# A chunked scan and a bilinear feed-forward on one core: the order of the first loads, the first products and some small work changed

## The chip, the core and the metric

The kernel runs on one core of one Trainium2 chip. A core has five engines with queues of their own: PE (TensorE, matrix products, with its weight loads shown as PEld), DVE (VectorE), ACT (ScalarE), POOL (GpSimd) and SP (SyncE, which here only issues transfers). Instructions of one engine start in the order of its queue; between engines they wait on semaphores. Transfers (DMAs) issued by POOL go through one queue, those issued by SP and ACT through two others, and the same 16 DMA engines serve all three. The metric is the device time of one execution in microseconds (us), and the median over several executions is compared.

## The reference

The inputs are x (4 batches, 8 heads, 768 tokens, 32 values), a decay a per token and head, and B and C (16 values per token and head). A state space scan is computed in chunks, then a feed-forward with two products and an elementwise product between them:

```python
for c in range(nc):
    cum = np.cumsum(la, axis=-1)                       # la = log a, of the chunk
    L = np.exp(cum[:, :, :, None] - cum[:, :, None, :]) * causal
    CB = np.einsum('bhin,bhjn->bhij', Cc, Bc)
    y_intra = np.einsum('bhij,bhjd->bhid', CB * L, xc)
    y_inter = np.einsum('bhin,bhnd->bhid', Cc, state) * np.exp(cum)[..., None]
    y[:, :, sl] = y_intra + y_inter
    ...
    state = decay_full * state + sum_j(B_j x_j decay_from_j)
x = y.transpose(0, 2, 1, 3).reshape(B * S, H * D)      # 3072 x 256
return (x @ w_a) * (x @ w_b) @ w_out                   # 256 -> 1536 -> 256
```

## The kernel before, in words

The kernel works in chunks of 128 tokens: six blocks (0 to 5) of 128 tokens, and in each block two pairs of batches, so that pair p = 2 x block + 0 or 1. All orders are written out by hand: the Python code records instructions in the order in which every engine is to run them, and each engine takes its own of them in that order. The program's end (lines 768 to 1026) is that order.

The decay of a chunk is a running product Pr (`scan`, L237, DVE), taken relative to its value in the middle of the chunk (`over_mid`, L240; `sel_over_mid`, L243). The factors that B and C are multiplied with come from it in three ways:

- Block 0: small products on PE (`factors_mm`, L258) that turn Pr, then a reciprocal on DVE into fB. `scale_bc` (L328) multiplies B and C into bm and cm, `transposes` (L372) turns them on PE, and ACT and DVE copy them out (L383, L388).
- Block 1 on (C and B in tiles cq and bq, loaded by `load_q`, L155): `mid_rows` (L275) makes Ps, `turned_rows` (L284, a DVE transpose) turns it into Pt, `batch_factors` (L290, copies on ACT) spreads it by batch into FC, and `batch_inverse` (L296, a DVE reciprocal) makes FB. `scale_q` (L341, POOL) writes C times FC or B times FB into one of three planes; `prep(p)` does both, C first. `turn` (L354, DVE) transposes a plane. Here the second index of FC and FB counts blocks from 1.
- The bm that the state needs in later blocks use fBl, made by `late_factors` (L300, L301).

For each pair, `scores` (L400) makes the products of C and B on PE in the four PSUM banks SC; `mask` multiplies them with the causal table, either on DVE (L445) or, by_pool, as a copy tmp on ACT (L442) and a product on POOL (L443). The products with x (scaled to f16 by `scale_x`, L315 on ACT or L317 on POOL) give y: `pv_u` and `pv1` (L454) for pairs 0 and 1, `outputs` (L533, L481, L469) later. `ds_mm` (L508, L497), `state_sums` (L567, L569) and `spread` (L573, L583) carry the state on.

The feed-forward of block 0 goes pair by pair. A unit (`unit_mm`, L595) makes products of 256 columns with Wa into a bank aps and with Wb into a bank bps; ACT copies aps out to asb (`evac_a`, L609), and DVE multiplies (`times`, L619) into hk. `out_mm` (L634) multiplies hk with Wo, and ACT copies the result out (L646). From block 1 on a unit covers four batches: `bunit` (L664, L676, hkb) and `bout` (L690, L702). The banks of PSUM that the units take are read one by one from the string BANKS (L22 to L25), four of them, numbered 0 to 3.

The loads: SP and ACT issue a, and B and C of pairs 0 and 1 (L185 to L195). POOL issues, one after the other, x of pair 0 (two transfers), the first half of Wa, the first half of Wb, x of pair 1 (two transfers), the second half of Wa (L220 to L226), later the second half of Wb and both halves of Wo (`load_wo`, L180), with other work of POOL between them. SP issues cq and bq of block 1 once the first half of Wa has landed (L814), then B of pairs 2 and 3, x of pairs 2 and 3 (after the first half of Wo, L857), then cq and bq of block 2 and so on. Each of its transfers also waits for the one issued eight before it.

While PE has nothing to do in the head, `warmup` (L230) puts in products of zeros: six of 512 columns and two of 128 at the very start (L768, L769), ahead of `factors_mm`, and a few at later places.

Of the kernel before, what the change touches and what calls it, by code (L numbers as in the profile page):

```python
# [19 lines left out]
YS = 16.0  # L20

BANKS = (  # L22
    "012313123123123012301230123021032110321032103210321031230120312031230213012301203213021302"
    "1301203120312031201320132013201320132013201320312031203120312031203120312031203120312"
)  # L25

# [2 lines left out]
def kernel(  # L29
# [13 lines left out]
    nc = tc.nc  # L43

    nb, H, S, D = x.shape
# [14 lines left out]
    NT = NBLK - PJ // NBP  # L60
# [102 lines left out]
    def load2(eng, p, which):  # L163
        if p < P2:
            return [load1(eng, p, which, bt) for bt in range(2)]
        blk, bp = divmod(p, NBP)
        src = (B, C, x)[which][2 * bp : 2 * bp + 2, :, blk * Q : (blk + 1) * Q, :]
        return [
            eng.dma_start(
                by_token(pair_in[p][which]).rearrange("p t h n -> p (t h) n"), src.rearrange("t h q n -> q (t h) n")  # L170
            )
        ]

    def load_w(half, W):
        src = moe_w_a if W is Wa else moe_w_b
        c = slice(half * KC, (half + 1) * KC)
        return nc.gpsimd.dma_start(W[half], src.rearrange("(f p) e -> p f e", p=128)[:, :, c])

    def load_wo(half):
        return nc.gpsimd.dma_start(  # L180
            Wo[:, 6 * half : 6 * half + 6].rearrange("p (g kk) e -> p g (kk e)", kk=3),
            moe_w_out.rearrange("(g p kk) e -> p g (kk e)", p=128, kk=3)[:, 2 * half : 2 * half + 2],
        )
# [36 lines left out]
    for p in range(2):  # L220
        for bt in range(2):
            load1(nc.gpsimd, p, 2, bt)
        if p == 0:
            w0 = load_w(0, Wa)
            load_w(0, Wb)
    load_w(1, Wa)  # L226

    def warmup(n, bank, cols=512):
        for _ in range(n):
            nc.tensor.matmul(  # L230
                bank[:, 0:cols], warm[:, 0:128], warm[:, 0:cols], start=True, stop=True, skip_group_check=True
            )
# [50 lines left out]
    def turned_rows(lo, hi):  # L283
        nc.vector.transpose(  # L284
            Pt[:, lo:hi].rearrange("p k s c -> p (k s) c"), Ps[:, lo:hi].rearrange("p k (i s) -> p k s i", s=4)
        )

    def batch_factors(lo, hi, *bs):
        for b in bs:
            nc.scalar.copy(  # L290
                FC[32 * b : 32 * b + 32, lo:hi].rearrange("p k s h -> p (k s) h"),
                Pt[:, lo:hi].rearrange("p k s (b h) -> p (k s) b h", b=nb)[:, :, b],
            )
# [25 lines left out]
    def scale_bc(p, which, eng, factor=None):  # L319
        blk, bp = divmod(p, NBP)  # L320
        name, f = (("bm", fB), ("cm", fC))[which]
        if p >= P2:
            f = (fBl, fCl)[which][:, blk - P2 // NBP].rearrange("p (b t h) -> p b t h", b=NBP, t=2)[:, bp]
        else:
            f = f[:, blk, :, bp]
        raw = by_token(pair_in[p][which]) if p >= P2 else pair_in[p][which].rearrange("p h r n -> p r h n")
        m_ = mid.tile([128, 2, H, N], f16, name=name, tag=name)
        eng.tensor_tensor(  # L328
            out=m_,
            in0=raw,  # L330
            in1=(f if factor is None else factor).unsqueeze(3).broadcast_to((128, 2, H, N)),
            op=ALU.mult,
        )
        st.setdefault(p, {})[name] = m_
# [59 lines left out]
    def scores(p):  # L394
        s = st[p] if p < PJ else st["U", p]
        BT, CT = s["BT"], s["CT"]
        s["T1"] = mid.tile([128, 4, 4, Q], f16, name="t1", tag="t1")

        def score(o_, b_, c_, at):
            nc.tensor.matmul(o_, b_, c_, start=True, stop=True, skip_group_check=True, tile_position=at)  # L400

        if p >= P2:
            for j, b in itertools.product(range(4), range(nb)):
                rows = slice(32 * b, 32 * b + 32)
                score(SC[b][:, j * Q : j * Q + Q], BT[rows, j], CT[rows, j // 2], (32 * b, 0))
            return
        for e, r, m, bt in itertools.product(range(2), range(2), range(4), range(2)):
            c0 = (e * 2 + r) * Q
            o_ = SC[m][64 * bt : 64 * bt + 64, c0 : c0 + Q]
            if p >= PJ:  # L410
                bp, g = divmod(m, 2)
                row = 32 * (2 * bp + bt)
                rows = slice(row, row + 32)
                b_ = BT[rows, 2 * g + e].rearrange("p (i r) -> p r i", r=2)[:, r]
                score(o_, b_, CT[rows, g], (row, 64 * bt))
            else:
                rows = slice(32 * m, 32 * m + 32)
                score(o_, BT[rows, e, r, bt], CT[rows, bt], (32 * m, 64 * bt))
# [72 lines left out]
    def ds_mm(p, DS):  # L491
        s, bp = st[p], p % NBP
        st["DS", p // NBP] = DS
        DS = DS.rearrange("p (g d) -> p g d", d=2 * D)
        for bt, g in itertools.product(range(2), range(4)) if p >= P2 else ():
            row = 32 * (2 * bp + bt)
            nc.tensor.matmul(  # L497
                DS[row : row + 32, g],
                s["bm"][:, bt, 2 * g : 2 * g + 2, :].rearrange("p h n -> p (h n)"),
                by_token(s["X16"])[:, bt, 2 * g : 2 * g + 2].rearrange("p h d -> p (h d)"),  # L500
                start=True,
                stop=True,
                skip_group_check=True,
                tile_position=(0, row),
            )
        for r, g, bt in itertools.product(range(2), range(4), range(2)) if p < P2 else ():
            k, row = slice(64 * bt, 64 * bt + 64), 32 * (2 * bp + bt)
            nc.tensor.matmul(  # L508
                DS[row : row + 32, g],
                s["bm"][k, r, 2 * g : 2 * g + 2, :].rearrange("p h n -> p (h n)"),  # L510
                s["X16"][k, 2 * g : 2 * g + 2, r, :],
                start=(r == 0 and g == 0),
                stop=(r == 1),
                skip_group_check=True,
                tile_position=(64 * bt, row),
            )
# [106 lines left out]
    def unit(p, k2, between=None, by_pool=False):  # L623
        a_ps = unit_mm(p, k2, Wa)
        if between:
            between()
        b_ps = unit_mm(p, k2, Wb)
        asb = evac_a(a_ps)
        return lambda: times(p, k2, b_ps, asb, by_pool)
# [92 lines left out]
    def go(*items):  # L722
        for p, k2 in items:
            unit(p, k2)()

    def prep(p):
        if p < NP:
            scale_q(p, 1, nc.gpsimd)
            scale_q(p, 0, nc.gpsimd)
# [35 lines left out]
    def bu(blk, *ks):  # L765
        return [lambda k=k: bunit(blk, k) for k in ks]

    warmup(6, SC[3])  # L768
    warmup(2, SC[3], 128)  # L769
    scan(0, 1)  # L770
    over_mid(0, 1)
    sel_over_mid(0, 1, nc.vector)
# [37 lines left out]
    scale_bc(1, 1, nc.vector)  # L810
    scan(4, 5)
    load_w(1, Wb)
    c3 = load_wo(0)
    for i_ in load_q(nc.sync, 1):  # L814
        tc.add_manual_dep(i_.ins, w0.ins.name, AFTER, reason="first weights ahead of block 1")
    for p in (2, 3):
# [35 lines left out]
        stop=True,  # L852
        skip_group_check=True,
    )
    load_wo(1)
    for p in (2, 3):
        for x_ in load2(nc.sync, p, 2):  # L857
            tc.add_manual_dep(x_.ins, c3.ins.name, AFTER, reason="weights and pair 3 ahead of x")
    loads_q(2)
    loads_b(4, 5)  # L860
    times(0, 0, bps[0], asb[0])
# [6 lines left out]
        in1=par.unsqueeze(1).unsqueeze(1).broadcast_to((128, H // 2, NG, 2)),  # L868
        op=ALU.mult,
    )  # L870
    ds_mm(0, SC[0][:, 0:256])
    bps.append(unit_mm(0, 2, Wb))
    for k2 in range(1, 3):
        times(0, k2, bps[k2], asb[k2])
    batch_inverse(0, 1)
    nc.vector.reciprocal(flat(fB, 1, 2), fps[:, 2 * NBP * H : 4 * NBP * H])
    prep(2)
    prep(3)
    go((1, 0), (1, 1), (1, 2))
    state_sums(0)  # L880
    spread(0)
    for p in (2, 3):
        scale_bc(p, 0, nc.gpsimd)
    go((0, 3), (0, 4), (1, 3))
    turn(2)
    turned_rows(1, NT)
    nc.gpsimd.memset(causal_q, 1.0)
    nc.gpsimd.affine_select(
        out=causal_q, in_=causal_q, compare_op=ALU.is_ge, fill=0.0, base=0, pattern=[[1, Q]], channel_multiplier=-1
    )  # L890
    go((0, 5))
    h = unit(1, 4, lambda: scores(2))
    turn(3)
    h()
    mask(product(2, 3), by_pool=True)
    mask(product(2, 0))
    h5 = unit(1, 5)
    batch_factors(1, NT, 0, 1)
    mask(product(2, 2), by_pool=True)
    mask(product(2, 1))  # L900
    o = [bank("ops"), bank("ops")]
    out_mm(0, 0, o[0], range(6))
    out_mm(0, 1, o[1], range(6))
    h5()
    scores(3)
    mask(product(3, 3), by_pool=True)
    batch_factors(1, NT, 2, 3)
    for m in range(3):
        mask(product(3, m))
    batch_inverse(1, NT)  # L910
    for bt in range(2):
        o.append(bank("ops"))
        out_mm(1, bt, o[-1], range(6))
# [17 lines left out]
        out_mm(p, bt, o[c], range(6, NK))  # L931
        out_store(p, bt, o[c])
    spread(1)
    bgo(1, 0, 1, 2, 3)

    scores(4)
    mask(product(4, 3), by_pool=True)
    prep(6)
    for m in range(3):
        mask(product(4, m))  # L940
        if m == 1:
            turn(5)
        bgo(1, *range(4 + 3 * m, min(7 + 3 * m, NK)))
# [113 lines left out]
```

## Time and profile before

| | us |
|---|---|
| median of 3 runs | 128.56 |
| lowest and highest of them | 127.66, 129.8 |
| the profiled execution, its own time | 128.17 |
| its span on the core | 126.5 |
| PE busy in the span | 118.3 (94%) |
| DVE, ACT, POOL busy | 90.3 (71%), 71.1 (56%), 55.2 (44%) |

The profile is of one execution. Its span runs from the first to the last instruction of the core; the execution's time has 1.7 us around it. Times in the views are counted from the start of the span. In a group of instructions "L609 ACT COPY asb<-aps" is line 609, engine ACT, a copy of aps into asb. A wait "A <- B" says that A's engine stood still until B was done. Where an instruction waits for several things, the profile names the one that came last by its records, which can be another than the one that mattered. The granted clock (PEclk) is the share of PE's full speed; DMA is the mean busy share of the 16 DMA engines.

### The profile page before, as it was taken

The page shows a single profiled execution, that of the slowest core. Times are in us where ns is not written, and L with a number is a line of the kernel's source. Part 1 is how long each engine was busy: PE and PEld are TensorE (multiplying, and loading weights), DVE is VectorE, ACT ScalarE, POOL GpSimd, SP SyncE. Part 2 cuts the span into 40 slices and gives each one's busy share as a digit, 9 for nine tenths or more (in the row PEclk, how much of TensorE's full clock was granted, in tenths as well). Part 3 has the DMA queues.
Part 4 walks back from the last instruction along what each step waited for, and adds up shares of the span by engine and source line. Part 5 has one row for each costly group of instructions (what it writes and reads, how often), then busy time and mean ns, then how long its engine had stood idle before and what let it go on. Part 6 is the DMA issues. An engine that isn't in the chain of part 4 may idle for free.

```text
span 126.5 us, 3575 instructions
## 1 busy us (share of the span) xinstructions
PE 118.3 (94%) x1389; PEld 75.3 (60%) x1389; DVE 90.3 (71%) x167; ACT 71.1 (56%) x142; POOL 55.2 (44%) x81
## 2 busy tenths in 40 slices
PE   6999589968999999999999999999999999999990
PEld 2546368957774447864448546558464675555880
DVE  4886865979778999559996789869689543747100
ACT  0464655645776768468765673572736545656220
POOL 7986730299867523728790499464000000000000
PEclk9999977999999999999999999999999999999999
DMA  3999999567797599669996599011101012010122
GB/s 67 174 169 229 200 206 202 96 141 161 108 125 130 126 112 156 99 99 120 160 178 210 143 122 144 16 44 41 47 3 41 0 47 83 0 41 0 41 98 73
DMA packets 55873, 13.44 MB, mean 106 GB/s; under 512 B 50896, under 2 KB 55632, under 8 KB 55856
## 3 DMA queue, kind: packets, MB, share of 16 engines
q1 hardware_dynamic: 51424, 9.71, 45.5%
q0 software_dynamic: 1904, 3.15, 14.1%
q10 hardware_dynamic: 2528, 0.36, 1.8%
q8 instruction: 11, 0.18, 0.7%
q14 instruction: 6, 0.05, 0.1%
HBM read 12.42 MB, written 3.15 MB: 123 GB/s over the span
## 4 chain that ended last, share of the span: by engine, by line
PE 71%; DMA 9%; SPq 7%; POOL 4%; DVE 3%; issue 2%; ACT 2%; POOLq 0%; ACTq 0%
PE ops L690 21%; PE aps L664 21%; PE bps L664 21%; SPq L155 7%; DMA Wa<-in_moe_w_a_dram 5%; DMA bn<-in_B_dram 4%; PE SC L400 3%; PE SC L469 2%; PE ops L634 2%; POOL xn L147 1%; POOL planes L341 1%; DVE t L445 1%; ACT x L315 1%; DVE Pt L284 1%; PE SC L533 1%
## 5 line engine op out<-in xcount | busy, mean ns | idle before, releaser
L609 ACT COPY asb<-aps 128x512 f32<-128x512 f32 x72 | 42.2, 587 | 17.8 <-PE aps L664 13.0
L676 DVE TENSOR_TENSOR hkb<-bps,asb 128x512 f16<-128x512 f32 x60 | 40.1, 685 | 12.5 <-ACT asb L609 10.9
L664 PE MATMUL aps<-XB,Wa 128*128 128x512 f16 x120 | 35.8, 379 | 0.0
L664 PE MATMUL bps<-XB,Wb 128*128 128x512 f16 x120 | 35.7, 379 | 0.0
L690 PE MATMUL ops<-Wo,hkb 128*128 128x256 f16 (+1 forms) x252 | 28.1, 268 | 0.0
L690 PEld LDWEIGHTS <-hkb 128*128 128x128 f16 x252 | 23.0, 98 | 3.8
L664 PEld LDWEIGHTS <-Wb 128*128 128x128 f16 x120 | 12.4, 103 | 13.7 <-issue 0.3
L664 PEld LDWEIGHTS <-Wa 128*128 128x128 f16 x120 | 12.1, 103 | 11.7 <-issue 0.5
L445 DVE TENSOR_TENSOR t<-SC,causal_q 128x512 f16<-128x512 f32 x27 | 17.3, 680 | 2.3 <-PE SC L400 2.3
L702 ACT ACTIVATE osb<-ops 128x256 f32<-128x256 f32 (+1 forms) x20 | 7.6, 379 | 17.7 <-PE ops L690 17.6
L443 POOL TENSOR_TENSOR t<-tmp,causal_q 128x512 f16<-128x512 f32 x5 | 5.8, 1158 | 13.6 <-ACT tmp L442 12.3
L341 POOL TENSOR_TENSOR planes<-cq,FC 128x256 f16<-128x256 f32 x10 | 7.7, 773 | 7.2 <-DMA bn<-in_B_dram 6.9
L619 DVE TENSOR_TENSOR hk<-bps,asb 128x512 f16<-128x512 f32 x12 | 8.1, 678 | 2.1 <-ACT asb L609 1.2
L341 POOL TENSOR_TENSOR planes<-bq,FB 128x256 f16<-128x256 f32 x10 | 7.7, 772 | 2.4 <-DMA bq<-in_B_dram 2.2
L595 PE MATMUL bps<-X2T,Wb 128*128 128x256 f16 x48 | 8.0, 298 | 0.0
L595 PE MATMUL aps<-X2T,Wa 128*128 128x256 f16 x48 | 8.0, 298 | 0.0
L442 ACT COPY tmp<-SC 128x512 f32<-128x512 f32 x10 | 5.9, 589 | 3.4 <-PE SC L400 3.1
L317 POOL TENSOR_SCALAR x<-xn 128x512 f16<-128x512 f32 x5 | 7.5, 1492 | 0.4
L555 ACT ACTIVATE XB<-SC 128x512 f16<-128x512 f32 (+1 forms) x10 | 5.1, 552 | 4.1 <-PE SC L497 2.4
L445 DVE TENSOR_TENSOR t<-SC,causal 128x512 f16<-128x512 f32 x11 | 6.9, 680 | 0.6 <-PE SC L400 0.4
L230 PE MATMUL SC<-warm 128*128 128x512 f16 (+1 forms) x15 | 5.3, 502 | 1.2 <-DVE warm L197 1.2
L354 DVE STREAM_TRANSPOSE turned<-planes 128x384 f32<-128x384 f32 x10 | 5.4, 560 | 1.1 <-POOL planes L341 1.1
(100 smaller groups left out, 112.3 us busy)
## 6 DMA issues: line engine op xcount, KB each, us to landing
out_dram<-osb SPq DMA_DIRECT2D x23, 128.0 KB, 1.7
xn<-in_x_dram SPq DMA_DIRECT2D x7, 256.0 KB, 5.1
cq<-in_C_dram SPq DMA_DIRECT2D x20, 64.0 KB, 4.2
bq<-in_B_dram SPq DMA_DIRECT2D x20, 64.0 KB, 3.6
bn<-in_B_dram SPq DMA_DIRECT2D x8, 128.0 KB, 4.2
Wa<-in_moe_w_a_dram POOLq DMA_DIRECT2D x2, 384.0 KB, 8.4
Wb<-in_moe_w_b_dram POOLq DMA_DIRECT2D x2, 384.0 KB, 8.7
Wo<-in_moe_w_out_dram POOLq DMA_DIRECT2D x2, 384.0 KB, 9.5
```

What stands on the lines that cost most here:

```text
L155: eng.dma_start(by_batch[blk][w][32 * b : 32 * b + 32].rearrange("i h s n -> i h (s n)"), (B, C)[w][b, :, blk * Q : (blk + 1) * Q, :].rear ...
L317: eng.tensor_scalar(xo, xi, XS, None, ALU.mult)
L341: eng.tensor_tensor(out=plane[:, c0 : c0 + 4 * step].rearrange("p (j c) s -> p j s c", c=step)[:, :, :, 0:N], in0=by_batch[blk][which][:, ...
L442: nc.scalar.copy(tmp, i_)
L445: nc.vector.tensor_tensor(out=o_, in0=i_, in1=c_, op=ALU.mult)
L595: nc.tensor.matmul(ps[:, kk * 2 * Q : (kk + 1) * 2 * Q], W[k // 6][:, f, k % 6 // 3 * 384 : (k % 6 // 3 + 1) * 384].rearrange("p (c kk) -> ...
L609: (nc.vector.tensor_copy if on_dve else nc.scalar.copy)(asb, a_ps)
L619: eng.tensor_tensor(out=s["hk"][:, 2 * k2 : 2 * k2 + 2, :].rearrange("p k q -> p (k q)"), in0=b_ps, in1=asb, op=ALU.mult)
L664: nc.tensor.matmul(t_, W[k // 6][:, f, k % 6 // 3 * 384 : (k % 6 // 3 + 1) * 384].rearrange("p (c kk) -> p kk c", kk=3)[:, k % 3], XB[:, b ...
L676: return lambda: nc.vector.tensor_tensor(out=s["hk"][:, k], in0=ps[1], in1=asb, op=ALU.mult)
L690: nc.tensor.matmul(o_ps[:, 0:w], hk[:, k, c * Q : (c + 1) * Q], Wo[:, k, cs], start=(k == 0), stop=(k == NK - 1), skip_group_check=True,)
L702: nc.scalar.activation(out=o_sb[:, 0:w], in_=o_ps[:, 0:w], func=AF.Copy, scale=1.0 / (YS * YS))
```

## The change

- In the head, the 6 products of 512 columns and 2 of 128 become 50 of 128.
- The first half of Wb is issued behind x of pair 1 instead of ahead of it.
- The first half of Wo is issued by POOL behind Ge instead of behind the second half of Wb; the second half behind the C rows (`scale_q`, which 1) of pairs 2 and 3. These two pairs' rows are made C, C, B, B instead of C, B, C, B. x of pairs 2 and 3 no longer waits for the first half of Wo.
- `turned_rows`, `batch_factors` and `batch_inverse` of blocks 2 to 5, one piece each before (32x512 and 128x128), are done for block 2 alone at the old place, and for blocks 3 to 5 among the units of block 1, there with the copies on POOL.
- In block 1, `turn(3)` goes behind the first mask of pair 2 on DVE, POOL's bm of pairs 2 and 3 and the table causal_q go behind POOL's masks, and the copies into FC behind ACT's second tmp of pair 2. `prep(6)` goes behind the first mask of pair 4.
- Some banks of the string BANKS are exchanged.

```diff
-    "012313123123123012301230123021032110321032103210321031230120312031230213012301203213021302"
+    "012313123123123012301230123021302113021031230120321031230120312031230213012301203213021302"
@@
             load1(nc.gpsimd, p, 2, bt)
         if p == 0:
             w0 = load_w(0, Wa)
-            load_w(0, Wb)
+    load_w(0, Wb)
     load_w(1, Wa)
@@
-    def batch_factors(lo, hi, *bs):
+    def batch_factors(lo, hi, *bs, eng=None):
         for b in bs:
-            nc.scalar.copy(
+            (eng.tensor_copy if eng else nc.scalar.copy)(
@@
-    warmup(6, SC[3])
-    warmup(2, SC[3], 128)
+    warmup(50, SC[3], 128)
@@
     load_w(1, Wb)
-    c3 = load_wo(0)
@@
-    load_wo(1)
     for p in (2, 3):
-        for x_ in load2(nc.sync, p, 2):
-            tc.add_manual_dep(x_.ins, c3.ins.name, AFTER, reason="weights and pair 3 ahead of x")
+        load2(nc.sync, p, 2)
@@
+    load_wo(0)
     ds_mm(0, SC[0][:, 0:256])
@@
-    prep(2)
-    prep(3)
+    scale_q(2, 1, nc.gpsimd)
+    scale_q(3, 1, nc.gpsimd)
+    load_wo(1)
+    scale_q(2, 0, nc.gpsimd)
+    scale_q(3, 0, nc.gpsimd)
     go((1, 0), (1, 1), (1, 2))
     state_sums(0)
     spread(0)
-    for p in (2, 3):
-        scale_bc(p, 0, nc.gpsimd)
     go((0, 3), (0, 4), (1, 3))
     turn(2)
-    turned_rows(1, NT)
+    turned_rows(1, 2)
+    go((0, 5))
+    h = unit(1, 4, lambda: scores(2))
+    h()
+    mask(product(2, 3), by_pool=True)
+    mask(product(2, 0))
+    turn(3)
+    h5 = unit(1, 5)
+    mask(product(2, 2), by_pool=True)
+    mask(product(2, 1))
+    scale_bc(2, 0, nc.gpsimd)
+    o = [bank("ops"), bank("ops")]
+    out_mm(0, 0, o[0], range(6))
+    out_mm(0, 1, o[1], range(6))
+    batch_factors(1, 2, 0, 1)
+    h5()
+    scores(3)
+    mask(product(3, 3), by_pool=True)
+    batch_factors(1, 2, 2, 3)
+    scale_bc(3, 0, nc.gpsimd)
     nc.gpsimd.memset(causal_q, 1.0)
     nc.gpsimd.affine_select(
...
-    go((0, 5))
-    h = unit(1, 4, lambda: scores(2))
-    turn(3)
-    h()
-    mask(product(2, 3), by_pool=True)
-    mask(product(2, 0))
-    h5 = unit(1, 5)
-    batch_factors(1, NT, 0, 1)
-    mask(product(2, 2), by_pool=True)
-    mask(product(2, 1))
-    o = [bank("ops"), bank("ops")]
-    out_mm(0, 0, o[0], range(6))
-    out_mm(0, 1, o[1], range(6))
-    h5()
-    scores(3)
-    mask(product(3, 3), by_pool=True)
-    batch_factors(1, NT, 2, 3)
     for m in range(3):
         mask(product(3, m))
-    batch_inverse(1, NT)
+    batch_inverse(1, 2)
@@
     spread(1)
-    bgo(1, 0, 1, 2, 3)
+    bgo(1, 0, 1)
+    turned_rows(2, NT)
+    batch_factors(2, NT, *range(nb), eng=nc.gpsimd)
+    bgo(1, 2, 3)
 
     scores(4)
     mask(product(4, 3), by_pool=True)
-    prep(6)
     for m in range(3):
         mask(product(4, m))
+        if m == 0:
+            batch_inverse(2, NT)
+            prep(6)
```

## The prediction

> **What bounds the kernel now.** I read the page's slices first (PE busy, clock, DMA), then the chain that ended last, then the waits and the timeline of the stretch that they point at. From 31 us to the end the chain is one unbroken run of PE products, so the time is set by when PE gets there; what can be won lies before 31 us.
>
> The page, the granted clock in 40 slices of 3.16 us, and three stretches of 3.41 us (busy us of PE, PEld, DVE, ACT, POOL; then clock, DMA share, GB/s):
>
> ```profile
> PEclk9999977999999999999999999999999999999999
> 13.75:17.16 3.41, 1.47 (x71) 1.13 (x69) 2.11 (x5) 1.57 (x6) 2.84 (x3) 1.00 1.15 199
> 17.16:20.57 3.41, 3.41 (x18) 2.42 (x17) 2.50 (x6) 1.41 (x7) 0.25 (x1) 0.50 1.27 216
> 20.57:24.00 3.43, 3.43 (x33) 3.24 (x32) 2.44 (x5) 2.34 (x4) 0.00 (x0) 1.00 0.90 152
> ```
>
> PE is busy for 1.47 of 3.41 us, and in the next 3.41 us its clock is 0.50. The waits between 10 and 31 us (total, times, longest):
>
> ```profile
> POOL planes L341 <- DMA bn<-in_B_dram: 6.9, 1, 6.9
> PEld L454 <- ACT x L315: 2.0, 1, 2.0
> PE SC L454 <- ACT x L315: 1.9, 1, 1.9
> PEld L400 <- DVE turned L354: 1.3, 1, 1.3
> ACT x L315 <- DMA xn<-in_x_dram: 1.3, 1, 1.3
> ```
>
> The 1.9 us are the products of pair 1 (L454), waiting for x of pair 1: issued at 6.2 us, it takes 9.3 us to land (15.5). POOL's 6.9 us are put down to bn, but the instruction reads cq of block 1, whose last piece is issued at 12.03 and takes 12.3 us (24.3). The chain there:
>
> ```profile
> 19.75 4.60 DMA bn<-in_B_dram
> ...
> 24.50 0.72 POOL planes L341
> ...
> 25.40 0.77 POOL planes L341
> ...
> 26.69 1.07 DVE Pt L284
> ...
> 30.64 0.71 PE SC L400 x32
> ```
>
> So C rows of pair 2 on POOL at 24.50, B rows at 25.40, turn(2) on DVE at 26.19, scores(2) on PE at 26.82, after 0.99 us of idle PE. All five moves aim at this.
>
> **The head.** The six products of 512 columns and two of 128 take 2.96 us from 1.25, and the factor products follow at 4.13 (their selr is ready at 3.70). Rows of 128 columns start 107 ns apart before 6.9 us, and 56 ns apart once the clock is up (four transposes at 11.12 to 11.29). Fifty take 5.33 us at 107 and 2.80 at 56, so the factor products come at 6.58, or 4.05 at best: later by 0 to 2.45 us. I take 2.45, since the 128-column rows up to 6.7 us are all at 107. Everything behind (fB, bm, cm, scores(0), masks, X2T) is one chain and shifts with it: X2T, done at 10.50, is done at 12.95. So the first Wa product starts at 12.95 instead of 10.66, where it waited for Wa (10.62). The Trainium skill (TensorE: Matmul & The Clock Gate, Part 1) says that warming takes a stretch of time of about 3.4 us and no number of products. By that rule narrow ones warm nothing sooner, and a warm stretch that began early would shorten the fifty; the 107 and 56 ns agree with it.
>
> **x of pair 1 ahead of Wb.** POOL's transfers land in order: Wa 10.62, Wb 12.8, x 15.5, second Wa 17.1, second Wb 19.4 (issue plus time to landing), a weight about every 2.2 us. With x in front, Wb lands between 12.8 and 15.5; I take 17.1 - 2.2 = 14.9, since the same bytes go ahead of the second Wa. x lands at about 12.7. The loss is hidden by the late head: transposes(1) and scores(1), at 12.31 now, come at 14.62 (2.29 later, like the Wa products), their masks at 15.3 to 17.2, POOL's mask (1.16 us behind ACT's tmp) at 17.36. PE does the two Wb units from 15.2 to 16.1 and idles until x (ACT, 17.2) and masks are there: pv1 at 17.3 instead of 16.27, 1.03 later. Idle PE is then 0.7 us in place of 1.95.
>
> **The clock.** From 17.13 to 20.50 sixteen products of 256 columns run 213 ns apart, against 109 later: 16 x 0.104 = 1.66 us lost. In 24.0 to 27.4 PE stands 0.99 us and the clock stays up, so 0.7 us should do no harm. PE is then ready for scores(2) at 25.83 + 1.03 - 1.66 = 25.2. The skill's page asks for an idle stretch of about 3.4 us before the clock falls. By that rule it would not have fallen after 1.95 us; the trace differs, and decides.
>
> **Both Wo later.** Wo0 is issued at 10.68 and Wo1 at 16.01; they land at 21.6 and 24.1. The pieces of cq land at 18.8, 21.2, 23.5 and 24.3, the first three of bq at 24.6, 24.8 and 25.0: eight small loads held back by the weights, the last five within 0.9 us of Wo1's end. Now Wo0's issue stands behind Ge (which waits for ACT's G, behind pv1), near 18.6, and Wo1 behind the C rows of pairs 2 and 3. Without Wo1 the backlog drains at 21.6 + 2 x 0.22 = 22.1 for cq and 23.0 for bq (0.22 us a piece, as those five); if the weights' queue runs dry after the second Wb (19.4), cq is there at 20.1. At no gain it is 24.3. With 22.1: C rows 22.2 and 22.8, Wo1's issue 0.75 (23.6 to 24.3), B rows of pair 2 at 24.35 to 25.1, turn(2) 0.58, scores(2) at 25.8. With 20.1 the B rows wait for bq and PE's 25.2 is the later. I take the middle, 25.5: **-1.3**. Behind Wo1's issue on POOL stand both B rows, spair and gV. Wo0 (first used at 28.7) and Wo1 (34.9) keep 3 us and more; x of pairs 2 and 3 lost its wait for Wo0 (21.6), which did not bind, as SP reached it at 25.05.
>
> **Side work behind masks.** scores(3) starts 3.82 us after scores(2), at the end of DVE's mask (30.59). DVE loses 0.68 there (the transpose of 32x512, 1.07, becomes 32x128, 0.39) but its hk now waits for PE's Wb unit (1.2 us after scores(2)): 1.2 + 0.65 + 0.6 + 0.55 + 0.6 = 3.6, **-0.2**. The two FC copies ahead of ACT's x shrink from 0.30 to 0.21 each and POOL's bm go behind its masks: the products at 33.86, which waited for x (33.81), gain **0.17**. DVE's reciprocal 0.94 becomes 0.34, in idle time.
>
> **Later.** In block 1 DVE gets a transpose 32x384 (between 0.39 and 1.07: 0.84) and a reciprocal 128x96 (0.34 to 0.94: 0.74); POOL four copies of 32x96 (between hr's 0.19 and the 1.03 of 32x512: 0.34 each, 1.4 in all), ahead of the mask of pair 4 and prep(6), where POOL idles 3.6 us from 45.9. DVE idles some 0.8 us from 39 to 44, so up to 0.8 us of 1.58 reaches PE. The new banks take away the wait of 0.17 at 39.20 (Wb unit on a bank still read by hkb) and let unit 7, not 6, wait for hkb of unit 4. I take **-0.17** and **+0.3** (bounds 0 and 0.8).
>
> **Sum.** -1.3 - 0.2 - 0.17 - 0.17 + 0.3 = -1.54. The profiled execution took 128.17 us (span 126.5 and 1.7 around it): 126.6. That execution lies 0.4 under the median of 128.56; against the median the forecast is 1.5% less.
>
> **Rivals.**
> - *The loads come early and the head is short.* If the clock rises some 1.4 us sooner, pv1 starts at 16.1 (Wb at 14.9 sets it), PE is ready at 25.83 - 0.17 - 1.66 = 24.0, and with B rows done by 23.4 scores(2) starts there: -2.8 in place of -1.3, 125.1. For it: the queue may run dry at 19.4. Against: POOL's C rows, Wo1's issue and bq all have to fit before 23.4.
> - *The clock falls all the same.* Late head plus 0.7 us idle look idle enough: PE is ready at 25.2 + 1.66 = 26.9, scores(2) is where it was, and only -0.24 of the rest stays: 127.9. The threshold lies between 1.47 busy of 3.41 (fell) and about 2.4 (stayed); here some 2.6.
> - *Slower: Wo1's issue delays the B rows.* If cq lands no sooner than 24.3, C rows 24.5 and 25.1, issue 25.9 to 26.6, B rows 26.65, turn(2) 27.45, scores(2) 28.05: +1.25 and -0.24, 129.2. It decides from cq at about 23.0 on; past 131.1 it needs cq 1.9 us later than today. For it: cq was slow already before Wo moved at all (issued at 10.6, landed 18.8). The Trainium skill (DMA: Bandwidth & Descriptors, Queues, rings and completion order) lets each DMA engine take turns between queues, packet by packet. By that rule cq has its turns beside Wo and would gain little from its absence. The five pieces landing right behind Wo1 speak against.
>
> **How the numbers follow.** Forecast 0.46 (its own range 125.7 to 127.6, from scores(2) at 25.2 to 25.8 and the DVE bound), early loads 0.22, clock falls 0.18, slower 0.14. 2% of the median is 2.57 us, about what a measurement of this kernel can tell from no change: under 126.0 or over 131.1. Faster: all of the early case but a tenth (0.20) and a third of the forecast's (0.15): 0.35. Slower: half of the last (0.07). Within: 0.58. The range 124.8 to 129.3 reaches over all four and leaves 0.2 at its ends.
>
> **What the profile after would show.** The factor products at 5 to 6.6 us; first Wa product near 12.9; no PE wait of 1.9 us at L454; granted clock 1.00 from 17 to 21; the last of cq landing before 23; scores(2) near 25.5; hkb on DVE without PE waiting more than 0.3 us near 43. I am wrong if the clock is 0.50 anywhere from 13 to 25, if cq lands after 23, or if PE waits for hkb for over 0.8 us.

## The result, and the profile after

The kernel after takes 126.9 us (median of 10 executions, 126.26 to 131.7), the kernel before, run beside it on the same chip, 128.53 (127.16 to 129.8). The ratio is 0.989, with a 95% interval from 0.9845 to 0.9938: 1.1% less time, within the 2% that count as no change. The forecast was 126.6. The ratios here and below leave out executions more than about 1.5% above the fastest of their kernel, so they can differ from the quotient of two medians (most for b_narrow, where three of six are left out). The profiled execution after took 126.51, with a span of 124.8; that is 1.66 less than the profiled one before (128.17), where the sum had 1.54.

The granted clock of the page, and the three stretches that the prediction read (the columns as there: length, busy us of PE, PEld, DVE, ACT and POOL, the clock, the DMA share, GB/s):

```profile
PEclk9999999999999999999999999999999999999999
13.75:17.16 3.41, 2.69 (x59) 2.07 (x64) 3.30 (x9) 3.26 (x7) 1.68 (x4) 1.00 1.22 214
17.16:20.57 3.41, 3.41 (x88) 2.98 (x88) 3.12 (x7) 2.31 (x8) 3.39 (x7) 1.00 0.78 131
20.57:24.00 3.43, 3.43 (x34) 3.25 (x32) 3.00 (x5) 2.32 (x5) 3.15 (x6) 1.00 1.12 181
```

PE is busy for 2.69 of the 3.41 us in which it had been busy for 1.47, and the clock stays at 1.00. In the second line 88 PE instructions run where 18 ran before, and POOL has 3.39 us of work in place of 0.25: it no longer stands and waits for cq.

The waits after, from 10 to 31 us (total, times, longest):

```profile
PEld L454 <- ACT x L315: 1.3, 2, 0.7
...
PEld L400 <- DVE turned L354: 0.6, 2, 0.4
PE SC L454 <- DVE t L445: 0.6, 1, 0.6
```

The 1.9 us of PE at L454 have become 0.6, and it is a mask of DVE that ends them, not x. POOL's 6.9 us at L341 are not in the list any more. The chain that ended last, after:

```profile
1.25 5.51 PE SC L230 x50
...
24.11 0.69 DVE hk L619
24.80 0.50 DVE turned L354
25.34 0.68 PE SC L400 x32
...
37.29 0.67 DVE hkb L676
...
39.25 0.66 DVE hkb L676
```

No transfer stands in it. It begins with the fifty products of the head (5.51 us), so what makes the head longer now lies on the way to the end. turn(2) (24.80) comes right behind a product of the feed-forward (24.11) on DVE, so B rows of pair 2 (on POOL at 21.16) were there before DVE was free. But from 36.7 to 44.6 us the chain passes through DVE, most of it hkb, where before it had been PE alone from 33.86 us on.

The starts of the same stages, and the landings, read from the instructions and transfers of the two traces:

| us from the span's start | before | after |
|---|---|---|
| factor products / first Wa product | 4.13 / 10.67 | 6.69 / 12.85 |
| x of pair 1, second transfer landed | 15.50 | 12.31 |
| first Wb, second Wa, second Wb landed | 12.8, 17.1, 19.4 | 13.5, 16.4, 19.4 |
| Wo0 and Wo1 issued | 10.7 and 16.0 | 18.4 and 20.4 |
| Wo0 and Wo1 landed | 21.6 and 24.1 | 23.3 and 27.4 |
| four pieces of cq landed | 18.8, 21.2, 23.5, 24.3 | 16.7, 17.0, 17.2, 17.5 |
| four pieces of bq landed | 24.6 to 25.2 | 19.6 to 20.2 |
| products of pair 1 with x | 16.27 | 17.10 |
| scores(2) | 26.82 | 25.34 |
| scores(4) | 40.59 | 38.70 |
| scores of the next pair | 48.14 | 46.45 |

From 48 us to the end the kernel after stays 1.69 ahead. The gain is made by 25 us (1.48) and up to scores(4) (1.89), and 0.20 of it is lost again by 48 us.

### The profile page after: what moved, and what is told of

It is laid out like the page before. It is cut to its first block, busy times and chain, and to the rows that moved or that the text cites. A ratio compares the mean times of both kernels' runs of the same rounds, so it can differ in the third digit from the quotient of the medians.

```text
span 124.8 us, 3665 instructions
## 1 busy us (share of the span) xinstructions
PE 118.4 (95%) x1431; PEld 78.5 (63%) x1431; DVE 89.7 (72%) x169; ACT 70.4 (56%) x142; POOL 56.1 (45%) x85
## 3 DMA queue, kind: packets, MB, share of 16 engines
q0 software_dynamic: 1904, 3.15, 14.7%
## 4 chain that ended last, share of the span: by engine, by line
PE 80%; DVE 11%; issue 3%; ACT 3%; ACTq 0%
PE ops L690 22%; PE aps L664 19%; PE bps L664 18%; PE SC L230 4%; DVE t L445 4%; PE SC L400 4%; PE ops L634 3%; DVE hkb L676 3%; PE aps L595 3%; PE bps L595 2%; PE SC L469 2%; ACT bt L383 1%; DVE hk L619 1%; DVE turned L354 1%; PE SC L533 1%
## 5 line engine op out<-in xcount | busy, mean ns | idle before, releaser
L609 ACT COPY asb<-aps 128x512 f32<-128x512 f32 x72 | 42.1, 586 | 16.4 <-PE aps L664 13.1
L676 DVE TENSOR_TENSOR hkb<-bps,asb 128x512 f16<-128x512 f32 x60 | 39.8, 682 | 11.6 <-ACT asb L609 10.7
L664 PEld LDWEIGHTS <-Wa 128*128 128x128 f16 x120 | 12.1, 103 | 11.9 <-issue 0.8
L445 DVE TENSOR_TENSOR t<-SC,causal_q 128x512 f16<-128x512 f32 x27 | 17.3, 679 | 2.3 <-PE SC L400 2.3
L443 POOL TENSOR_TENSOR t<-tmp,causal 128x512 f16<-128x512 f32 x5 | 5.8, 1156 | 6.9 <-ACT tmp L442 6.3
L341 POOL TENSOR_TENSOR planes<-cq,FC 128x256 f16<-128x256 f32 x10 | 7.5, 770 | 1.7 <-DMA cq<-in_C_dram 1.5
L230 PE MATMUL SC<-warm 128*128 128x128 f16 (+1 forms) x57 | 6.9, 311 | 1.2 <-DVE warm L197 1.2
L341 POOL TENSOR_TENSOR planes<-bq,FB 128x256 f16<-128x256 f32 x10 | 7.5, 769 | 1.0 <-DMA bq<-in_B_dram 1.0
L230 PEld LDWEIGHTS <-warm 128*128 128x128 f16 x65 | 6.3, 137 | 1.9 <-DVE warm L197 1.2
L595 PE MATMUL bps<-X2T,Wb 128*128 128x256 f16 x48 | 7.1, 273 | 0.0
```

What stands on the lines that cost most here:

```text
L230: nc.tensor.matmul(bank[:, 0:cols], warm[:, 0:128], warm[:, 0:cols], start=True, stop=True, skip_group_check=True)
L341: eng.tensor_tensor(out=plane[:, c0 : c0 + 4 * step].rearrange("p (j c) s -> p j s c", c=step)[:, :, :, 0:N], in0=by_batch[blk][which][:, ...
L443: nc.gpsimd.tensor_tensor(out=o_, in0=tmp, in1=c_, op=ALU.mult)
L445: nc.vector.tensor_tensor(out=o_, in0=i_, in1=c_, op=ALU.mult)
L595: nc.tensor.matmul(ps[:, kk * 2 * Q : (kk + 1) * 2 * Q], W[k // 6][:, f, k % 6 // 3 * 384 : (k % 6 // 3 + 1) * 384].rearrange("p (c kk) -> ...
L609: (nc.vector.tensor_copy if on_dve else nc.scalar.copy)(asb, a_ps)
```

## Experiments

Three questions were open: which of the five moves makes the gain, whether it comes from the clock or from the loads, and whether something behind scores(2) eats what is won. Twelve kernels were run in three groups of four, each group beside the kernel before; the medians of before were 128.58, 128.15 and 128.21. Ratios are to the before of the same group. A profile is one execution: the landing of the same load differs between profiles (the second transfer of x of pair 1 landed at 15.50 in before and at 14.12 in b_fill, with the loads in the same order), so a start read in one profile is weaker evidence than a median.

### One part of the change undone, or done alone

**a_wide**: the short head back.

```diff
-    warmup(50, SC[3], 128)
+    warmup(6, SC[3])
+    warmup(2, SC[3], 128)
```

> The kernel after, with the first products as before (6 of 512 columns and 2 of 128 instead of 50 of 128). Theory, in two parts: the gain of 1.6 us comes from C and B of block 1 landing before PE wants them, and from the clock that stays up; the fifty products only make the head 2.2 us later, and that is hidden as long as PE would wait for Wb (13.5) anyway. Then here the first Wa product comes at 10.8, PE waits for Wb until 13.5, the products of pair 1 start near 15.0 instead of 17.1, and scores(2) comes 0.3 to 2 us sooner than 25.3: 125.0 to 126.5. Rival 1, the fifty products keep the clock up: granted clock 0.50 for 3.4 us between 13 and 25 us, and 127.5 to 128.5. Rival 2, the late head is what leaves the weights' queue empty (POOL issues the second Wb 2.2 us later) so that cq gets through: cq lands after 19 us instead of 17.5, and scores(2) stays at 25.3 or comes later: 126.9 or more.

Measured: 126.55 (125.75 to 127.42), ratio 0.9875 (0.9813 to 0.9937). The factor products came at 4.13, but the first Wa landed only at 11.66 and the first Wb at 15.32 in this execution, so the products of pair 1 came at 16.67 and scores(2) at 24.85: 0.49 sooner than after. At scores(4) 0.18 of that was left, and the span is 124.9, as after. The waits from 28 to 40 us hold two lines that bear on it:

```profile
DVE turned L354 <- POOL planes L341: 1.0, 1, 1.0
...
PE aps L664 <- DVE hkb L676: 0.2, 1, 0.2
```

turn(4) (34.28) waits for the B rows of pair 4, which start on POOL at 33.48. Two things came just before that: bq of block 2 landed at 33.27, and V on DVE, which the profile names, ended at 33.28. hkb stands behind turn(4).

**a_woearly**: both Wo issued at their old places.

```diff
     load_w(1, Wb)
+    load_wo(0)
...
+    load_wo(1)
     for p in (2, 3):
         load2(nc.sync, p, 2)
...
-    load_wo(0)
     ds_mm(0, SC[0][:, 0:256])
...
     scale_q(3, 1, nc.gpsimd)
-    load_wo(1)
```

> The kernel after, with both halves of Wo issued at their old places (behind the second Wb, and behind pair 1's work on POOL), rows still C, C, B, B. Theory: bq is held back by Wo as before, its last piece lands near 24 to 25 instead of 20.2, the B rows start there instead of at 21.2, scores(2) comes at 25.8 to 26.3 instead of 25.3: 127.4 to 128. Rival, the DMA engines take turns between the queues, and it was the gap behind the second Wa that let the loads through: cq and bq land by 21, scores(2) at 25.3: 126.9.

Measured: 127.04 (125.95 to 129.76), ratio 0.9882 (0.9807 to 0.9957). cq landed at 17.9 to 21.3 and bq at 21.7 to 22.7: later than after, sooner than before. In the profiled execution the clock rose at 3.99, not at 6.70, and the narrow head was 1.26 shorter for it; scores(2) came at 24.36, behind 0.45 us of idle PE, 0.98 sooner than after. The gain was gone by 48 us (0.20 behind after): PE stood 0.69 us for hkb at 37.61. So in the kernel after, Wo at its old place costs nothing that the ratio shows. In two of the six executions the mean clock was below 0.99 (129.15 and 129.76).

**a_xlate**: the first Wb ahead of x of pair 1 again.

```diff
             w0 = load_w(0, Wa)
-    load_w(0, Wb)
+            load_w(0, Wb)
```

> The kernel after, with the first half of Wb issued ahead of x of pair 1 again. Theory: with the late head nothing waits for either; ACT's scaling of x comes at 16.3, and x lands at 13.5 to 15.5; so 126.9, scores(2) at 25.3. Rival, x in front is what saves the wait: x lands past 16, PE idles 2 us ahead of the products of pair 1, the clock falls to 0.50: 128 or more.

Measured: 126.35 (125.85 to 127.68), ratio 0.9885 (0.9809 to 0.9961). scores(2) at 25.37, 0.03 from after; the clock stays up. x lands at 14.58, still 0.9 sooner than before, and PE's idle time ahead of the products of pair 1 is 0.62 us, as after. This profile is of the slowest of the six executions: bq of block 2 landed at 34.32 (32.69 after), PE stood 0.70 us for hkb at 38.62, and by 48 us it was 1.21 behind after.

**b_narrow**: the kernel before with the fifty narrow products alone (the diff of a_wide, reversed).

> The kernel before, with the 50 products of 128 columns alone. Theory: the head comes 2.2 us later, the wait for x of pair 1 shrinks from 1.9 to under 1 us and the clock stays up, but bq still lands at 24 to 25 behind Wo, so scores(2) stays at 26.3 to 26.9 and the time within 0.5 us of the kernel before (128.0 to 128.6). Rival, the fifty products carry the gain: 126.9.

Measured: 127.82 (125.83 to 129.54), ratio 0.9888 (0.9799 to 0.9977). The factor products came at 6.69, the products of pair 1 at 17.25, and the clock did not fall. POOL reached the issues of the second Wb and of Wo0 later (12.31 and 13.05 in place of 9.95 and 10.68), behind those of cq, and the pieces of cq landed at 17.9 to 19.0. Those of bq still stood behind Wo: 21.0, 23.3, 24.5, 25.6. PE was idle for 1.89 us ahead of scores(2) at 27.22. So in this profile the late head lets cq through and the clock stays up, but scores(2) waits for the other half of its rows. What the narrow head is worth alone stays unclear: the quotient of the two medians is 0.994, the profiled execution (128.41) is slower than the median, and in one of the six the mean clock was 0.985.

No single part, taken away, costs what the whole brings, so the parts can stand in for one another. The next four kernels asked for the reason.

### The clock alone, Wo alone, and the work behind scores(2)

**b_fill**: before, with PE kept busy in the first gap.

```diff
+    warmup(30, fps[:, 256:], 128)
     load_wo(1)
```

> The kernel before, with 30 products of zeros of 128 columns added on PE right ahead of the products of pair 1 with x (L454), where PE stood idle for 1.95 us; no load is moved. Theory A (the clock is the gain): PE stays busy, the clock stays at 1.00 from 17 to 21 us in every execution, and the time is that of the one execution of the kernel before whose mean clock was 1.0: 126.9. Theory B (the loads are the gain): cq still lands at 24.3, the B rows of pair 2 end at 26.1, scores(2) stays near 26.8, and PE only idles longer ahead of it (0.99 + 1.66 = 2.6 us): 128.2 to 128.5. If 2.6 us of idle PE at 24 to 27 lower the clock in their turn, 129.5 or more.

Measured: 128.14 (127.06 to 129.53; 12 executions), ratio 0.9974 (0.9927 to 1.002). In the profiled execution scores(2) came at 26.28, behind 2.29 us of idle PE, and the clock fell there instead:

```profile
19.35:22.76 3.41, 3.41 (x34) 3.23 (x32) 3.00 (x5) 2.31 (x5) 0.78 (x1) 1.00 1.26 202
22.76:26.17 3.41, 1.23 (x12) 0.90 (x9) 1.22 (x3) 1.28 (x3) 1.31 (x3) 1.00 0.63 115
26.17:29.59 3.42, 3.31 (x43) 2.44 (x44) 3.25 (x6) 0.97 (x2) 3.35 (x9) 0.50 0.78 168
```

As before, the slow stretch lasts one stretch of 3.41 us and follows one in which PE was busy for little of its time. Six of the twelve executions had a mean clock of 0.995 or more and took 127.06 to 128.05; the other six, at 0.983 to 0.987, 128.22 to 129.53. Among the 17 executions of before in this group, six had 0.995 or more. Filling the first gap moves nothing on average; in the profile the wait for the loads moved the fall to the next gap.

**b_wo**: before, with both Wo later and nothing else.

```diff
-    c3 = load_wo(0)
...
-    load_wo(1)
     for p in (2, 3):
-        for x_ in load2(nc.sync, p, 2):
-            tc.add_manual_dep(x_.ins, c3.ins.name, AFTER, reason="weights and pair 3 ahead of x")
+        load2(nc.sync, p, 2)
...
+    load_wo(0)
     ds_mm(0, SC[0][:, 0:256])
...
-    prep(2)
-    prep(3)
+    scale_q(2, 1, nc.gpsimd)
+    scale_q(3, 1, nc.gpsimd)
+    load_wo(1)
+    scale_q(2, 0, nc.gpsimd)
+    scale_q(3, 0, nc.gpsimd)
```

> The kernel before, with only both halves of Wo issued later (Wo0 behind Ge, Wo1 behind the C rows of pairs 2 and 3, rows in the order C, C, B, B); the head, x of pair 1, the side work and the banks stay as they were. Theory B (the loads are the gain): the last of cq lands at 22 or sooner, bq at 23 or sooner, the B rows are done by 24.5, and PE, with its clock still down to 0.50 at 17 to 20.5, is the later: scores(2) at 25.8 in place of 26.8, 127.2 to 127.6. Theory A (the clock is the gain): with the clock down nothing is won, 128.5. Theory C (the DMA engines take turns between queues, so small loads gain nothing from Wo's absence): cq lands at 24 as before, Wo1's issue comes ahead of the B rows, 129.0.

Measured: 125.86 (125.55 to 127.03), ratio 0.9825 (0.9766 to 0.9885): as much as the whole change or more (the intervals overlap), and beyond every theory's number. The transfers issued by SP, from issue to landing (KB each, median us), in the stretch from 10 to 17 us:

```profile
cq<-in_C_dram SPq DMA_DIRECT2D x4, 64.0 KB, 8.0
bq<-in_B_dram SPq DMA_DIRECT2D x4, 64.0 KB, 6.5
```

Before, these were 11.1 and 10.6. cq landed at 18.8 to 19.7, right behind the second Wb (18.5), and bq at 20.0 to 20.9. All expectations had let the clock fall as before. It did not: all six executions had a mean clock of 0.996 or more. In the profile x of pair 1 and the second Wa, which are issued ahead of Wo0 in the same queue, also landed 0.8 and 1.2 sooner (14.7, 15.9), and PE's wait at L454 shrank from 1.95 to 1.09. That this is the doing of Wo is not shown: with Wo0 at its old place x landed at 14.1 in b_fill, and with Wo later at 15.2 in bw_late. Why the clock stays up so reliably with Wo later is open. scores(2) came at 23.64, 3.2 sooner than before. Of that, half was lost again by scores(4) (1.55 left). PE stood 0.51 us at 31.08, ahead of the products with x of pairs 2 and 3, and for the larger part the chain names where:

```profile
30.36 2.99 DMA bq<-in_B_dram
33.56 0.78 POOL planes L341
34.36 0.58 DVE turned L354
36.24 0.73 issue
36.97 0.64 DVE hkb L676
37.65 0.59 PE bps L664 x2
```

bq of block 2, the B rows of pair 4, turn(4), then the two late factors (34.86 to 37.05), and only then hkb, for which PE stands 1.25 us at 37.65.

**a_late** and **a_wide_late**: after, and a_wide, with the late factors moved into DVE's idle time.

```diff
     batch_inverse(1, 2)
+    late_factors()
...
     turn(4)
-    late_factors()
```

> The kernel after, with late_factors() (the two factors for blocks 3 to 5 on DVE) moved from behind turn(4) to ahead of it, right behind batch_inverse of block 1, into DVE's idle time at 32 to 33 us. Theory S (a second bound: the B rows of pair 4 wait on POOL for bq of block 2, and DVE's turn(4), which waits for them in order, holds up the two late factors and hkb behind it): DVE's work behind turn(4) gets shorter by the two factors, PE loses its breaks at the first units of block 1, and the time is 0.1 to 0.4 less than after, 126.5 to 126.8 where after gave 126.9. Rival (turn(4) is hidden, the slack of PE's banks covers it): no difference, 126.9; or slower by up to 0.3, if the two factors now delay turn(4) itself or the masks of pair 3.

Measured: 126.48 (125.68 to 126.84), ratio 0.9856 (0.9805 to 0.9908). It can't be told from after (0.9845 to 0.9938). The profiled execution shows neither theory cleanly: its x of pair 3 landed late (31.3), PE stood 1.09 us for it at 32.36, and bq of block 2 landed at 34.4.

> The kernel after with the short head of before (6 products of 512 columns and 2 of 128 in place of 50 of 128) and late_factors() ahead of turn(4). With the short head alone scores(2) came at 24.85 in place of 25.34, and the gain of 0.5 was gone again at the first units of block 1 (PE stood there, DVE's turn(4) at 34.3 behind bq of block 2). Theory S (that second bound ate it): part of the 0.5 is kept now, 126.0 to 126.3. Rival (the landing of bq of block 2 itself, 33.3, sets the pace, whatever stands behind turn(4)): 126.5 to 126.6 as with the short head alone.

Measured: 125.88 (124.65 to 127.55), ratio 0.979 (0.973 to 0.985). First Wa landed at 10.76 and first Wb at 13.37 here; scores(2) came at 23.30, 2.04 sooner than after, and at 46 us 0.90 of that was left. The time is below what either theory expected. By the medians it is 0.67 below a_wide, but the two ratios (0.979 and 0.9875) have intervals that overlap, and the two profiles differ from the first loads on (Wa at 10.76 against 11.66). That the moved factors keep a part of the gain here is likely, not shown.

### Wo alone with the late factors moved, and each other part on top

**bw_late**: b_wo with the diff of a_late.

> The kernel before with both halves of Wo later (125.86 by itself) and late_factors() ahead of turn(4). With Wo alone scores(2) came at 23.64, 3.2 sooner than before, but PE then stood 1.25 us at 37.65 for hkb, which DVE began at 36.97 behind turn(4) (34.36) and the two late factors (2.2 us). Theory S (those two factors ate what the loads had won): hkb begins at 35.0, the 1.25 are gone, 124.6 to 124.9. Rival (the factors now delay DVE's V by 0.75 and with it the scores of pair 4, or bq of block 2 lands too late anyway): 125.6 to 125.9.

Measured: 125.46 (124.69 to 125.82), ratio 0.9784 (0.9742 to 0.9826): the lowest ratio of the study, and lower than that of after, since the two intervals don't meet, though after was measured beside another set of before. scores(2) came at 24.17 in this execution, 0.5 later than in b_wo (x of pair 1 landed 0.5 later), and yet scores(4) came at 37.91 in place of 39.04: PE's 1.25 us at 37.65 are gone. From 31.35 us on the chain is one run of PE again:

```profile
31.35 0.78 PE SC L481 x55
32.45 2.07 PE ops L634 x18
34.52 0.43 PE aps L664 x2
38.31 0.55 PE aps L664 x2
```

**bw_late_x** (x of pair 1 ahead of the first Wb), **bw_late_n** (the fifty narrow products) and **bw_late_s** (side work, pieces and banks) each add one part of the change to bw_late.

> bw_late with x of pair 1 issued ahead of the first Wb as well. Theory R (behind a short head the order costs): Wb lands at 15 in place of 12.8, the two Wb units of pair 0 wait for it, the products of pair 1 with x start 0.5 to 1.2 later than without, and scores(2) with them: 0.5 to 1.0 slower than bw_late. Prediction's reading (x was what PE waited for, so x sooner is a gain): x lands at 12.5 in place of 14.7, the 1.1 us of idle PE at 15.5 go, 0.3 to 0.8 faster than bw_late.

Measured: 125.61 (124.99 to 127.54), ratio 0.9798 (0.9752 to 0.9844). x landed at 12.7, but PE then waited 0.56 us at 13.97 for the first Wb (13.92); the products of pair 1 came 0.5 sooner than in bw_late, scores(2) 0.5 sooner, the span is 123.2 against 123.8. In the medians no difference is left.

> bw_late with the head of 50 products of 128 columns. The factor products come up to 2.5 later, 1.2 where the clock rises early. Theory R (once the loads are early, PE's own work sets scores(2), so a late head is paid): scores(1) 1.2 to 2.5 later, the products of pair 1 1.0 to 1.6 later, 0.8 to 1.5 slower than bw_late. Rival (the late head hides in waits for the loads, as the prediction had it): the same as bw_late within 0.3.

Measured: 125.81 (125.28 to 126.53), ratio 0.9824 (0.978 to 0.9868). scores(2) came at 25.10, 0.93 later than in bw_late, and the span is 124.6, 0.8 longer: in the profile the late head is paid, as Theory R has it. In the medians it is 0.35, within the intervals.

> bw_late with the side work moved behind masks, the later factor rows in pieces on POOL and the exchanged banks, that is all of the change but the head and the order of x and Wb, with late_factors() ahead of turn(4). By the prediction's terms: 0.2 less to scores(3), 0.2 less for banks, 0.2 more for the pieces on DVE, 0.1 to 0.3 faster than bw_late. Rival (the side work brings nothing, since scores(2) and bq of block 2 set the pace, and the pieces on POOL and DVE cost): the same or up to 0.3 slower.

Measured: 125.86 (125.53 to 127.07), ratio 0.9845 (0.9795 to 0.9894). The span is that of bw_late (123.8), with PE standing 1.01 us at 31.14, ahead of the products with x of pairs 2 and 3. No gain shows; the medians differ by 0.4 the other way, within the intervals.

## Why the prediction came out right, step by step

The total and the range held, in part by luck. The kernel did not do it quite for the reasons given.

- *What bounds the kernel: right in place, one reading wrong.* The chain before is not PE alone from 31 us on: from 31.37 to 33.82 it stands on ACT (a mask's copy, FC and x), and PE is alone from 33.86. The prediction's own term of 0.17 lies there.
- *The head: right.* 5.33 us at 107 ns were forecast, 5.51 measured; factor products at 6.69 (6.58), first Wa product at 12.85 (12.95). The bound of 4.05 at a raised clock is real as well: where it rose at 3.99 the same fifty were 1.26 shorter. It is not free: after, the chain begins with it.
- *x of pair 1 ahead of Wb: place right, importance wrong.* The products of pair 1 came at 17.10 (17.3), with 0.62 us of idle PE (0.7). Wb landed 1.4 sooner than the 14.9 taken. But undoing it costs nothing that a_xlate shows. With the late head ACT wants x only at 16.33, and x landed at 14.58 there; even the 15.50 of before would have done, and b_narrow, with the old order of x and of Wo, has the same 0.62 us of idle PE.
- *The clock: right that it stays up, too simple in what that is worth.* 39 executions of before in the three groups fall into 13 with a mean clock of 0.995 or more (median 127.66) and 26 below 0.99 (median 128.58): some 0.9 go with it (1.1 and 0.7 within the two groups that have enough of both), not 1.66. And b_fill shows that filling the gap ahead of the products of pair 1 does not keep the clock up by itself. After the whole change nine of ten executions had a mean clock of 0.998 or more; the slowest (131.7) had 0.974.
- *The loads: right in direction, mis-sized.* The last of cq was put at 22.1, or 20.1 if the weights' queue ran dry; it landed at 17.5. (The five pieces behind Wo1, from which the 0.22 us a piece was taken, landed within 1.07 us of its end, 24.12 to 25.19, not 0.9; the step holds.) The late head made POOL issue the second Wb at 12.16, behind all four pieces of cq (10.78 to 12.13), and they landed between the second Wa (16.37) and it (19.38). The prediction moved the factor products by the late head but not this issue, which stands behind work of the head in POOL's order. The other profiles agree: with the second Wb issued at 11.9 or later (after, a_xlate, b_narrow, bw_late_n) all four pieces of cq landed 1.6 us or more ahead of it; at 10.9 or sooner (all other profiles) at most one was ahead of it. The middle between 25.2 and 25.8 for scores(2) came out near by luck: the loads stopped counting, and what was left was the engines' own pace, put at 25.2, at 25.34 (PE was idle for only 0.14 us there, and turn(2) ended at 25.30).
- *The rule of the Trainium skill behind the slower rival* (DMA: Bandwidth & Descriptors, Queues, rings and completion order: each DMA engine takes turns between queues), from which that rival drew that cq would gain little from Wo's absence: in b_wo the last five of the same eight loads land 4.3 to 4.7 us sooner than before, issued at most 2.2 us sooner. Turns there may be, but that conclusion from them does not hold here. The slower rival fell with it: after, the C rows began on POOL at 19.21 and Wo1's issue at 20.40, ahead of need.
- *Side work, copies, bank: 0.54 forecast, 0.41 measured* between scores(2) and scores(4). *Later work: +0.3 forecast, +0.20 measured.* These are differences of two profiles; bw_late_s, which adds these parts alone to bw_late, shows no gain. The transpose of 32x384, the reciprocal of 128x96 and POOL's copies were put at 840, 740 and 340 ns; in the groups of after (mean ns behind the comma):

```profile
L290 POOL COPY FC<-Pt 32x96 f32<-32x96 f32 x4 | 1.0, 257 | 0.1
L284 DVE STREAM_TRANSPOSE Pt<-Ps 32x384 f32<-32x384 f32 x1 | 0.8, 848 | 0.0
...
L296 DVE RECIPROCAL FB<-FC 128x96 f32<-128x96 f32 x1 | 0.7, 730 | 0.0
```

- *What failed is the sentence "All five moves aim at this", read as if each paid its share, and the carrying of a gain at scores(2) to the end at full value.* Wo's later issue alone is enough (b_wo), but it is not the only way: a_woearly, with all the rest and Wo early, has a ratio of 0.9882. The rest is not shown to add anything to Wo's later issue: bw_late with one more part is never shown to be faster, and with all of them (a_late) it is 126.48 to 125.46, in two groups whose ratios have intervals that barely overlap (0.9805 to 0.9908, 0.9742 to 0.9826). And what comes early at scores(2) meets a second bound at 33 to 37 us: bq of block 2, turn(4), the late factors, hkb. b_wo lost 1.6 of its 3.2 from scores(2) to scores(4), 1.25 of idle PE there; moving the late factors ahead of turn(4) took these 1.25 away (bw_late). Among the kernels after, those whose scores(2) came sooner or whose bq of block 2 landed later stood there too (a_woearly 0.69, a_xlate 0.70). In the profile of after itself PE has no such wait.

Of the signs that the prediction named, all came out but one by a little: the factor products at 6.69, where 5 to 6.6 was said.

The early rival (125.1) was right that the loads come early. That a short head is worth more is what the medians of a_wide (126.55) and a_wide_late (125.88) suggest, within overlapping intervals. It overlooked the second bound.

What stays open: why the clock stays up with Wo later, how much of the 0.35 and 0.4 by which the medians of bw_late_n and bw_late_s lie over bw_late is real, and what a version would give in which bq of block 2 lands sooner; that was not tried.

## What to carry to other kernels

When small loads that are due soon share the DMA engines with big ones that are due late, try first to issue the big ones later, and look at what that alone does before adding other moves. A gain early in a chain is worth what the next waiting engine in line lets through: follow the order of that engine's queue to the next thing that comes from a load. Several moves that each remove the same wait don't add up; do each alone, and undo each alone, to see it.

## What the runs showed of the hardware

*The clock falls by stretches.* The clock's records run in stretches of 3.41 us counted from its rise, and a stretch at 0.50 follows one with little PE work in it. Over the profiles of all kernels here, leaving out the programs' ends, PE's busy time in the emptiest such stretches was 1.23 (b_fill) and 1.47 (before), each followed by 0.50, and 1.53 (b_narrow), 1.64 (bw_late) and more elsewhere, followed by 1.00. For the two that stayed up:

```profile
24.14:27.56 3.42, 1.53 (x35) 1.21 (x37) 1.67 (x3) 1.24 (x3) 1.76 (x3) 1.00 0.63 120
27.56:30.97 3.41, 3.04 (x48) 2.58 (x37) 3.41 (x7) 2.25 (x5) 3.33 (x8) 1.00 0.68 149
```

```profile
14.13:17.54 3.41, 1.64 (x73) 1.42 (x72) 2.29 (x6) 1.72 (x8) 2.33 (x4) 1.00 1.18 210
17.54:20.96 3.42, 3.42 (x33) 3.05 (x31) 2.90 (x6) 2.36 (x5) 1.05 (x2) 1.00 1.06 160
```

The first fence is b_narrow, the second bw_late. A single idle time of 1.77 us lay inside the second's stretch and did no harm; 1.95 us in before's did. The programs' ends agree: last stretches with 0.3 to 0.9 us busy (six profiles) were followed by 0.50, and such with 1.6 to 1.8 (bw_late_x, a_woearly, a_late, b_fill) by 1.00. That the limit lies near 1.5 of 3.41 rests on the four stretches above, and was not tested by itself. The Trainium skill (TensorE: Matmul & The Clock Gate, Part 1), cited in the prediction, asks for an idle stretch of about 3.4 us. The traces differ: both falls inside the programs came with PE busy for more than a third of it.

*The rise varies.* With kernels whose first instructions are the same the clock rose at 6.70 (after) and at 3.99 and 4.03 (a_woearly, a_late), over all profiles from 3.9 to 7.2.

*Small loads land between weights.* The 64-KB pieces of cq and bq mostly land 0.2 to 0.4 us apart, in groups right behind the end of a weight, though another queue carries the weights. In most cases a piece lands ahead of a weight that was issued behind it and behind one that was issued ahead of it: in b_narrow, Wo0 is issued at 13.05, between the first piece of bq (12.80) and the second (13.30), and it lands at 23.14, between theirs (21.00 and 23.35). It is no strict rule: before, three pieces of bq were issued ahead of Wo1 (16.01) and landed behind it (24.12).
